# The last 64 tokens of two batches as one chunk of a gating product, with loads and splits in other places

## The chip, the cores and the metric

The kernel runs on one core of a Trainium2 chip. The metric is the device time of one execution in microseconds, as the median over several runs. Before the change it is 576.93 us (three runs, 575.62 to 577.12).

## What is computed

An attention (4 batches, 8 heads, 576 tokens, 64 dimensions, rotary embedding), then two feed-forward layers over the concatenated heads, in float32:

```python
attn = softmax(rot(q) @ rot(k).T / sqrt(64)); x = attn @ v        # (4, 576, 512)
h = gelu_tanh(x @ w_in)                                           # w_in (512, 1024)
u, v = h[..., :512], h[..., 512:]
v_n = (v - mean) / sqrt(var + 1e-6) * g_ln                        # per token
v_s = einsum('ts,bsd->btd', w_sg, v_n) + b_sg[None, :, None]      # mixes the 576 tokens
x2 = x + (u * v_s) @ w_out
gate = sigmoid(causal_conv5(x2) * conv_w)
out = (gate * (x2 @ w_val)) @ w_out2
```

The weights of both layers come as 64-bit floats, which the kernel narrows itself.

## The kernel before, in words

**Precision.** A product in float32 is made of three products of a faster type: each operand is split into a high part (a cast on ScalarE, ACT) and a low part (source minus high part, on GpSimd, POOL, or the Vector engine, DVE), and high x high, high x low and low x high are summed in PSUM. `split` (line 255) records such a pair, `tt` (line 246) one subtraction or product on DVE ("D") or POOL ("P"), `acopy` one cast.

**Order.** Nothing is emitted at once. `Plan.add` collects tasks with an engine, an estimated cost and the keys they read and write; `Plan.order` then runs a list scheduler over them, by due time, and emits the instructions in the order that it finds. Each engine takes its own instructions in that order, one after the other. TensorE's order is fixed by the order of recording. `after=` adds a dependence: `sp[i]` is the first TensorE task of pair i's phase, `mq[i]` the DMA that stores the row maxima of pair i. Loads and stores go through one queue, SP's.

**Attention** works on 16 pairs of heads, four per batch. `phase(i)` interleaves nine score units of pair i (exponentials on ACT, lines 495 to 508) with the nine score units for the maxima of pair i+1 (line 445, reduced by DVE on line 447 into `mx`, and on line 461 into `mn`). Behind it come the product with v (lines 526 and 536, read out as `xu`) and the sums of exponentials (line 562, read out by ACT as `ss`). `prep_high(i+2)` makes the rotary products on DVE (`raw`) and casts `qp`, `qh`, `kh` on ACT; `prep_low` makes `ql` and `kl` on POOL. The unnormalised result goes to `xu_d[i]` and the reciprocal sums to `r_d[i]` in DRAM.

Beside the pairs 4 to 14 lies what the next stage needs: `weights_a` loads eight pieces of w_in, narrows each with one ACT and four DVE operations (lines 295 to 302) and splits it, and splits five pieces of w_sg (`s_h`, `s_l`) that go through the buffers `xs`. `x_prep(0)`, from pair 13 on, loads four row blocks of x of batch 0 into `xs`, multiplies with the reciprocal sums (`rb`) on POOL, stores them as `x_d` and splits them into `XH`, `XL`. Two `xs` buffers serve in turn.

**Gating** (`part_a`, once per batch): v units, u units, g units.
- Three v units multiply chunks of 128 tokens of x with the right half of w_in (line 686): chunks 0 and 1, chunks 2 and 3, and one last chunk. 576 is 4 x 128 + 64, so the last chunk takes the last 128 tokens, of which the first 64 were done already. Each chunk costs 12 matmuls of 512 columns. Then gelu, the statistics (DVE, with one power on POOL), normalisation and the split into `vn`; of the last chunk only its upper 64 rows, as high and low part in the two halves of one tile `t4`.
- Four u units (line 725) do the left half, by blocks of 128 channels.
- Four g units (lines 739 and 742) do the mixing over tokens. DVE adds the bias (`vs`), POOL multiplies with u, and the result goes to `g_d`.

`x_prep(b + 1)` is recorded between the u and g units: `XH` and `XL` exist once, so the next batch's can only be written when the u units have read them.

**Second layer.** `x2_part` (line 804) makes x2 in tiles `xs` and `rb`, splits it (`xh2`, `xl2`) and runs the convolution (four DVE operations on line 822 per block). `val_part` (line 837) and `out_part` (line 866) follow, batch by batch.

Of the kernel before, what the change touches and what calls it, by code (L numbers as in the profile page):

```python
# [10 lines left out]
F32 = mybir.dt.float32  # L11
# [155 lines left out]
def mixer_kernel(ctx: ExitStack, tc: tile.TileContext, qk, v, vrem, cs, w_in, g_ln, w_sgT, b_sg,  # L167
# [42 lines left out]
    s_l = pA.tile([128, 5, S], F32R, name="s_l")  # L210
    WR = tiles(pA, "wr", 1, [128, 512, 2], I32)
# [107 lines left out]
    def weights_a():  # L319
        for hf in (1, 0):  # L320
            for k in range(4):
                cc = slice(512 * hf, 512 * hf + 512)
                weight64(f"win{k}_{hf}", lambda k=k, cc=cc: w_h[:, k, cc], lambda k=k, cc=cc: w_l[:, k, cc],
                         w_in[128 * k:128 * k + 128, 1024 * hf:1024 * hf + 1024], [mq[4 + nw[0]]])
# [6 lines left out]
        for k in range(5):  # L331
            xs = XS[k % 2][:, 4:]

            def ld(q, k=k, xs=xs):
                if k < 4:
                    q.dma_start(out=xs, in_=w_sgT[128 * k:128 * k + 128, :])
                else:
                    q.dma_start(out=xs[0:64], in_=w_sgT[512:576, :])
                    q.dma_start(out=xs[64:128], in_=w_sgT[512:576, :])
            dma(288, ld, w=[("xs", k % 2)], n=1 + (k == 4), after=[mq[5 + 2 * k]])  # L340
            split(lambda k=k: s_h[:, k], lambda k=k: s_l[:, k], lambda xs=xs: xs, S, [("xs", k % 2)],
                  ("sg", k, "h"), ("sg", k, "l"), after=[sp[5 + 2 * k]])
# [232 lines left out]
    sp = []  # L575
# [7 lines left out]
    def attention():  # L583
# [42 lines left out]
        for i in range(NPAIR):  # L626
# [26 lines left out]
    def x_prep(b):  # L653
        for hp in range(4):
# [4 lines left out]
            op = [mq[13 + hp // 2]]  # L659
# [9 lines left out]
            tt("P", xs, xs, lambda rb=rb: rb, ALU.mult, S, [("rb", hp % 2)], [kx], [sp[14]] if not b else ())  # L669
            dma(290, lambda q, xs=xs, i=i: q.dma_start(out=x_d[i], in_=xs()), [kx], [("x_d", i)])  # L670
            split(lambda hp=hp: XH[:, hp], lambda hp=hp: XL[:, hp], xs, S, [kx], ("X", hp, "h"), ("X", hp, "l"), "D")

    def part_a(b):
# [4 lines left out]
        for c0 in (0, 2, 4):  # L678
            cs_ = (c0, c0 + 1) if c0 < 4 else (4,)

            def mm(ps, cs_=cs_):
                for y, c in enumerate(cs_):
                    o = 128 * c if c < 4 else S - 128
                    for k in range(4):
                        for z, (p, q) in enumerate(three(3)):
                            nc.tensor.matmul(ps[:, y], X[p][:, k, o:o + 128], Wm[q][:, k, 512:1024], start=k == z == 0,  # L686
                                             stop=k == 3 and z == 2)
            ps, kp = unit(12 * 0.233 * len(cs_), mm, [*xk, *[(f"win{k}_1", m) for k in range(4) for m in hl]])
# [5 lines left out]
            for y, c in enumerate(cs_):  # L694
# [315 lines left out]
```

## Time and profile before

| | |
|---|---|
| median of three runs | 576.93 us |
| time of the profiled execution | 575.71 us |
| its span, first to last instruction | 573.8 us |
| TensorE (PE) busy | 560.6 us, 98% |
| DVE busy | 396.2 us, 69% |
| ACT busy | 277.0 us, 48% |
| POOL busy | 254.1 us, 44% |
| share of the chain that ended last: PE, DVE, DMA | 90%, 5%, 2% |
| stages: attention, gating, second layer | to 252, to 418, to the end |

Busy time says how long an engine had an instruction in work. Whether a saving on it is a saving of time is read from the chain: the work that ended last, followed back from the end, at each step to what released it. Idle time of an engine ahead of an instruction stands in brackets with its releaser.

### The profile page before, as it was taken

The page shows a single profiled execution, that of the slowest core. Times are in us where ns is not written, and L with a number is a line of the kernel's source. Part 1 is how long each engine was busy: PE and PEld are TensorE (multiplying, and loading weights), DVE is VectorE, ACT ScalarE, POOL GpSimd, SP SyncE. Part 2 cuts the span into 40 slices and gives each one's busy share as a digit, 9 for nine tenths or more (in the row PEclk, how much of TensorE's full clock was granted, in tenths as well). Part 3 has the DMA queues.
Part 4 walks back from the last instruction along what each step waited for, and adds up shares of the span by engine and source line. Part 5 has one row for each costly group of instructions (what it writes and reads, how often), then busy time and mean ns, then how long its engine had stood idle before and what let it go on. Part 6 is the DMA issues. An engine that isn't in the chain of part 4 may idle for free.

```text
span 573.8 us, 11977 instructions
## 1 busy us (share of the span) xinstructions
PE 560.6 (98%) x4682; PEld 470.4 (82%) x4682; DVE 396.2 (69%) x584; ACT 277.0 (48%) x448; POOL 254.1 (44%) x211
## 2 busy tenths in 40 slices
PE   7899999999999999999999999999999999999996
PEld 4677777677776676768989989989999989899985
DVE  5677777888889889726457665656568998837720
ACT  2565666666666666634425325325335453433321
POOL 5633333445545445564577477547453222220200
PEclk9899999999999999999999999999999999999999
DMA  5735556655656555553383472451513341220102
GB/s 210 205 95 133 149 140 194 190 127 170 183 158 182 156 149 153 179 152 115 100 283 106 153 245 79 155 166 39 178 62 125 104 138 39 81 94 1 38 37 93
DMA packets 53832, 76.79 MB, mean 134 GB/s; under 512 B 25104, under 2 KB 29712, under 8 KB 53776
## 3 DMA queue, kind: packets, MB, share of 16 engines
q1 hardware_dynamic: 53632, 76.03, 43.7%
q8 instruction: 37, 0.61, 0.4%
q14 instruction: 19, 0.16, 0.1%
q10 hardware_dynamic: 144, 0.00, 0.0%
HBM read 55.33 MB, written 18.95 MB: 129 GB/s over the span
## 4 chain that ended last, share of the span: by engine, by line
PE 90%; DVE 5%; DMA 2%; issue 1%; ACT 1%; POOL 0%; SPq 0%; DVEq 0%; ACTq 0%
PE ps L495 11%; PE ps L526 10%; PE ps L686 10%; PE ps L837 9%; PE ps L725 9%; PE ps L804 9%; PE ps L739 9%; PE ps L866 9%; PE ps L562 5%; PE ps L445 4%; PE ps L503 3%; DVE raw L249 2%; DVE mx L447 2%; PE ps L742 1%; PE ps L536 1%
## 5 line engine op out<-in xcount | busy, mean ns | idle before, releaser
L447 DVE TENSOR_REDUCE mx<-ps 128x2 f32<-128x576 f32 x128 | 91.1, 754 | 39.3 <-PE ps L445 21.7
L508 ACT ACTIVATE e<-ps 128x576 f32<-128x576 f32 x144 | 86.2, 651 | 25.8 <-PE ps L503 16.3
L250 POOL TENSOR_TENSOR ql<-raw,qh 128x576 fp32r<-128x576 f32 x15 | 21.7, 1445 | 101.3 <-ACT qh L253 68.2
L526 PE MATMUL ps<-e,vm 128*64 128x288 f32 x512 | 65.6, 409 | 0.0
L739 PE MATMUL ps<-s_h,vn 128*128 128x288 f32 x256 | 56.0, 294 | 0.0
L526 PEld LDWEIGHTS ps<-e,vm 128*64 128x64 f32 x512 | 35.4, 137 | 24.7 <-issue 2.5
L250 POOL TENSOR_TENSOR ac<-e,e 128x576 f32<-128x576 f32 x32 | 45.0, 1428 | 15.1 <-ACT e L508 15.1
L249 DVE TENSOR_TENSOR raw<-raw,cst 128x1152 f32<-128x1152 f32 (+2 forms) x35 | 43.2, 1243 | 6.5 <-DMA cst<-cs 6.5
L445 PE MATMUL ps<-kh,qp 64*128 64x288 f32 x256 | 39.2, 340 | 4.5 <-ACT qp L253 2.7
L739 PEld LDWEIGHTS ps<-s_h,vn 128*128 128x128 f32 x256 | 42.8, 188 | 0.0
L495 PE MATMUL ps<-qh,kh 64*128 64x288 f32 x256 | 39.2, 301 | 1.2 <-DVE mx L447 1.2
L250 POOL TENSOR_TENSOR vs<-vs,u 128x576 f32<-128x576 f32 x16 | 27.1, 1691 | 28.3 <-DVE vs L746 24.4
L495 PE MATMUL ps<-qh,kl 64*128 64x288 f32 x256 | 38.4, 295 | 0.0
L495 PE MATMUL ps<-ql,kh 64*128 64x288 f32 x256 | 38.4, 295 | 0.0
L495 PE MATMUL ps<-mr,one_r 64*128 64x288 f32 x256 | 38.3, 293 | 0.0
L445 PEld LDWEIGHTS ps<-kh,qp 64*128 64x128 f32 x256 | 22.9, 186 | 18.6 <-ACT qh L253 5.6
L725 PE MATMUL ps<-XH,w_l 128*128 128x288 f32 x128 | 37.8, 295 | 0.0
L837 PE MATMUL ps<-xh,wh_v 128*128 128x288 f32 x128 | 37.8, 295 | 0.0
L837 PE MATMUL ps<-xh,wl_v 128*128 128x288 f32 x128 | 37.8, 295 | 0.0
L739 PE MATMUL ps<-s_l,vn 128*128 128x288 f32 x128 | 37.7, 295 | 0.0
L725 PE MATMUL ps<-XL,w_h 128*128 128x288 f32 x128 | 37.7, 295 | 0.0
L837 PE MATMUL ps<-xl,wh_v 128*128 128x288 f32 x128 | 37.7, 295 | 0.0
(155 smaller groups left out, 1599.2 us busy)
## 6 DMA issues: line engine op xcount, KB each, us to landing
raw<-qk SPq DMA_DIRECT2D x31, 576.0 KB
xu_d<-xu SPq DMA_DIRECT2D x32, 144.0 KB
rb<-r_d SPq DMA_DIRECT2D x32, 144.0 KB
xs<-xu_d SPq DMA_DIRECT2D x16, 288.0 KB
x_d<-xs SPq DMA_DIRECT2D x16, 288.0 KB
g_d<-vs SPq DMA_DIRECT2D x16, 288.0 KB
vm<-v SPq DMA_DIRECT2D x16, 256.0 KB
wr<-w_in SPq DMA_DIRECT2D x8, 512.0 KB
```

The lines of the kernel that those rows point to most:

```text
L249: return add("DVE", dve(n), lambda: nc.vector.tensor_tensor(out_(), a(), b(), op), r, w, after, lock=True)
L250: return add("Pool", pool(n), lambda: nc.gpsimd.tensor_tensor(out_(), a(), b(), op), r, w, after, lock=True)
L445: nc.tensor.matmul(ps[:, h, 0:HALF], QP[j2][rows, c], kh[rows, cols], start=True, stop=True)
L447: add("DVE", 0.76, lambda: nc.vector.tensor_reduce(out=MX[j2][:, hk, :, c], in_=ps[:, :, 0:HALF], axis=AX.X, op=ALU.max), [kps], [("mx", j ...
L495: nc.tensor.matmul(ps[:, h, 0:HALF], x[rows, keys] if o < 3 else x[rows], y[rows, cols], start=o == 0, stop=o == 3)
L508: add("Act", 0.62, lambda: nc.scalar.activation(E[n], ps[:, :, 0:HALF], AF.Exp), [kps], [("e", n)])
L526: nc.tensor.matmul(pv[64 * hf:64 * hf + 64, h, 0:HALF], VM[j2][:, j, h], E[EU[i, us[hf]]][:, h], start=j == 0, stop=False, skip_group_chec ...
L686: nc.tensor.matmul(ps[:, y], X[p][:, k, o:o + 128], Wm[q][:, k, 512:1024], start=k == z == 0, stop=k == 3 and z == 2)
L725: nc.tensor.matmul(ps[:, hf, 0:HALF], Wm[p][:, k, dc], X[q][:, k, cols], start=k == z == 0, stop=k == 3 and z == 2)
L739: nc.tensor.matmul(ps[:, hf, 0:HALF], VN()[p][:, k, dc], SG[q][:, k, cols], start=k == z == 0, stop=False)
L804: nc.tensor.matmul(ps[:, hf, 0:HALF], w2("o", p)[:, k, dc], (T["gh"], T["gl_"])[q][j][:, k, cols], start=k == z == 0, stop=k == 3 and z == 2)
L837: nc.tensor.matmul(ps[:, hf, 0:HALF], w2("v", p)[:, k, dc], (T["xh2"], T["xl2"])[q][j][:, k, cols], start=k == z == 0, stop=k == 3 and z == 2)
```

## The change

- Batches 0 and 1 share one last v chunk of 128 tokens, the last 64 of each, and so do batches 2 and 3. It is multiplied in the even batch; the odd batch has two v units. Its operands are new tiles `XR` (high and low), made by `xr_prep`: eight loads of 128x64 from `xu_d`, sixteen of 64x64 of `r_d`, a product and a subtraction on POOL and a cast on ACT. `xr_prep(0)` runs beside the attention, `xr_prep(2)` within batch 0.
- `t4` becomes two tiles, one for each batch of the couple: four casts and two POOL subtractions in an even batch instead of two and one in each.
- The pieces of w_in are loaded from pairs 2, 3, 5, 6, 8, 9, 11, 12 instead of 4 to 11, those of w_sg from 4, 6, 7, 9, 10 instead of 5, 7, 9, 11, 13.
- `x_prep(0)` starts its row blocks from pairs 11, 12, 13 and 14 instead of 13, 13, 14 and 14.
- The low part of x2 is made by DVE in batches 0 and 1, and by POOL, as before, in batches 2 and 3.

```diff
+    XR = [pA.tile([128, 4, 128], F32R, name=f"xr_{nm}") for nm in "hl"]
+    RR = pA.tile([128, 4, 128], F32, name="rr")
...
-                         w_in[128 * k:128 * k + 128, 1024 * hf:1024 * hf + 1024], [mq[4 + nw[0]]])
+                         w_in[128 * k:128 * k + 128, 1024 * hf:1024 * hf + 1024], [mq[(2, 3, 5, 6, 8, 9, 11, 12)[nw[0]]]])
...
-            dma(288, ld, w=[("xs", k % 2)], n=1 + (k == 4), after=[mq[5 + 2 * k]])
+            dma(288, ld, w=[("xs", k % 2)], n=1 + (k == 4), after=[mq[(4, 6, 7, 9, 10)[k]]])
...
             phase(i)
+            ep.append(P.last_pe)
...
-            op = [mq[13 + hp // 2]]
+            op = [mq[11 + hp]]
...
-            split(lambda hp=hp: XH[:, hp], lambda hp=hp: XL[:, hp], xs, S, [kx], ("X", hp, "h"), ("X", hp, "l"), "D")
+            split(lambda hp=hp: XH[:, hp], lambda hp=hp: XL[:, hp], xs, S, [kx], ("X", hp, "h"), ("X", hp, "l"), "D", [ep[11 + hp]] if not b else ())
+
+    def xr_prep(b):
+
+        def f():
+            return XR[1].bitcast(F32)
+        for m in range(2):
+            for hp in range(4):
+                i, cc = 4 * (b + m) + hp, slice(64 * m, 64 * m + 64)
+                op = [] if b else [mq[9 + hp]]
+                dma(32, lambda q, i=i, hp=hp, cc=cc: q.dma_start(out=f()[:, hp, cc], in_=xu_d[i][:, 512:576]), [("xu_d", i)],
+                    [("xr", m, hp)], [*op, *P.readers.get(("XR", "l"), ())])
+
+                def ld(q, i=i, hp=hp, cc=cc):
+                    for h in range(2):
+                        q.dma_start(out=RR[64 * h:64 * h + 64, hp, cc],
+                                    in_=r_d[i][S * h + 512:S * h + S].partition_broadcast(64))
+                dma(32, ld, [("r_d", i)], [("rr", m, hp)], op, n=2)
+        parts = [(m, hp) for m in range(2) for hp in range(4)]
+        tt("P", lambda: RR, f, lambda: RR, ALU.mult, 512, [("xr", *x) for x in parts], [("rr", *x) for x in parts], [] if b else [sp[12]])
+        keys = [("rr", *x) for x in parts]
+        acopy(lambda: XR[0], lambda: RR, 512, keys, [("XR", "h")])
+        tt("P", lambda: XR[1], lambda: RR, lambda: XR[0].bitcast(F32), ALU.subtract, 512, [("XR", "h"), *keys],
+           [("XR", "l"), *[("xr", *x) for x in parts]], [] if b else [sp[13]])
...
-        for c0 in (0, 2, 4):
+        for c0 in (0, 2, 4)[:3 - b % 2]:
...
-                    o = 128 * c if c < 4 else S - 128
...
-                            nc.tensor.matmul(ps[:, y], X[p][:, k, o:o + 128], Wm[q][:, k, 512:1024], start=k == z == 0,
+                            nc.tensor.matmul(ps[:, y], X[p][:, k, 128 * c:128 * c + 128] if c < 4 else XR[p][:, k], Wm[q][:, k, 512:1024], start=k == z == 0,
...
+                    for m in range(2):
+                        own, other = slice(64 * m, 64 * m + 64), slice(64 - 64 * m, 128 - 64 * m)
+                        for rows in (own, other):
+                            acopy(lambda m=m, rows=rows: T4()[m][rows], lambda gi=gi, own=own: GL()[gi][own, 0], 512, [("gl", gi, y), kg],
+                                  [("vn", 4 + m, "h" if rows is other else "l")])
+                        tt("P", lambda m=m, own=own: T4()[m][own], lambda gi=gi, own=own: GL()[gi][own, 0],
+                           lambda m=m, own=own: T4()[m][own].bitcast(F32), ALU.subtract, 512, [("gl", gi, y), kg], [("vn", 4 + m, "l")])
...
+        if b == 0:
+            xr_prep(2)
...
-                  ("X2", j, dd, "h"), ("X2", j, dd, "l"))
+                  ("X2", j, dd, "h"), ("X2", j, dd, "l"), "D" if b < 2 else "P")
```

The scheduler makes a new order of all this. At three places it reads as follows.

ScalarE at the end of pair 13's phase, two before the last, before the change: the casts of the last pair (`qp`, `qh`, `kh`) with the readout `xu`, and `ss`, the readout of the sums.

```order
L253 CAST w_h<-wf_142 128x512
L508 ACTIVATE e_188<-ps_121 128x576
L253 CAST qp_160<-raw_146 128x512
L253 COPY xu_192<-ps_124 128x576
L253 CAST qh_147<-raw_146 128x576
L253 CAST kh_153<-raw_146 128x576
L566 ACTIVATE ss_193<-ps_123 128x288
L295 ACTIVATE wt_143<-wr_141 128x512
```

And the same place of the changed kernel:

```order
L297 ACTIVATE wt_201<-wr_199 128x512
L510 ACTIVATE e_191<-ps_121 128x576
L255 CAST qp_163<-raw_149 128x512
L255 COPY xu_195<-ps_124 128x576
L255 CAST qh_150<-raw_149 128x576
L255 CAST XH<-xs_133 128x576
L568 ACTIVATE ss_196<-ps_123 128x288
L255 CAST kh_156<-raw_149 128x576
L510 ACTIVATE e_183<-ps_124 128x576
```

A cast of x stands ahead of `ss`, and `kh` behind it.

DVE in the last phase with score units for a next pair (stretch 14 in the prediction), before: from the reduction on line 461 to the first reductions of the last pair.

```order
L461 TENSOR_REDUCE mn_174<-mx_172 128x8
L455 TENSOR_REDUCE mn_174<-ps_122 128x1
L249 TENSOR_TENSOR raw_146<-raw_146,cst 128x1152
L249 TENSOR_TENSOR raw_146<-raw_146 128x576
L249 TENSOR_TENSOR raw_146<-raw_146,cst 128x1152
L249 TENSOR_TENSOR raw_146<-raw_146 128x576
L300 SCALAR_TENSOR_TENSOR wt_198<-wr_196,wt_198 128x512
L302 SCALAR_TENSOR_TENSOR wf_197<-wr_196,wt_198 128x512
L447 TENSOR_REDUCE mx_173<-ps_121 128x2
```

The same place of the changed kernel:

```order
L463 TENSOR_REDUCE mn_177<-mx_175 128x8
L251 TENSOR_TENSOR raw_149<-raw_149,cst 128x1152
L457 TENSOR_REDUCE mn_177<-ps_122 128x1
L251 TENSOR_TENSOR raw_149<-raw_149 128x576
L251 TENSOR_TENSOR raw_149<-raw_149,cst 128x1152
L573 RECIPROCAL rc_197<-rc_197 128x9
L251 TENSOR_TENSOR raw_149<-raw_149 128x576
L251 TENSOR_TENSOR XL<-xs_134,XH 128x576
L251 TENSOR_TENSOR XL<-xs_133,XH 128x576
L449 TENSOR_REDUCE mx_176<-ps_121 128x2
```

Two subtractions of x take the place of the two weight operations, and a reciprocal has come between.

POOL in batch 0 of the gating, before: the last `vn` subtraction, t (the last 64 tokens' low part) and the first g product `vs`.

```order
L702 TENSOR_TENSOR st_3293<-st_3293,mhalf 128x1
L250 TENSOR_TENSOR vn_3285<-gl_3289,vn_3284 128x512
L250 TENSOR_TENSOR t_3286<-gl_3288,t_3286 64x512
L250 TENSOR_TENSOR wl_o<-wf_142,wh_o 128x512
L250 TENSOR_TENSOR vs_3290<-vs_3290,u 128x576
```

The same place of the changed kernel:

```order
L727 TENSOR_TENSOR st_3342<-st_3342,mhalf 128x1
L252 TENSOR_TENSOR vn_3333<-gl_3338,vn_3332 128x512
L252 TENSOR_TENSOR rr<-xr_l,rr 128x512
L252 TENSOR_TENSOR t_0_3334<-gl_3337,t_0_3334 64x512
L252 TENSOR_TENSOR t_1_3335<-gl_3337,t_1_3335 64x512
L252 TENSOR_TENSOR wl_o<-wf_145,wh_o 128x512
L252 TENSOR_TENSOR xr_l<-rr,xr_h 128x512
L252 TENSOR_TENSOR vs_3339<-vs_3339,u 128x576
```

The product and the subtraction for the chunk of batches 2 and 3 have come in, ahead of t and ahead of `vs`.

## Rows read from the trace of the kernel before

**Rows 1.** Busy time by stretch, the gating (columns as headed).

```profile
core 0: us, PE busy (x) PEld busy (x) DVE busy (x) ACT busy (x) POOL busy (x), PEclk, DMA share, GB/s
...
252.00:418.00 166.00, 166.00 (x1075) 155.46 (x1073) 97.78 (x160) 62.36 (x97) 98.37 (x78) 1.00 0.46 148
```

**Rows 2.** Chain that ended last, by time (start us, us, what): gating, second layer.

```profile
252.01 14.14 PE ps L686 x60
...
278.88 1.60 PE ps L739 x12
...
293.72 13.94 PE ps L686 x60
...
320.38 1.60 PE ps L739 x12
...
437.27 12.97 PE ps L837 x96
```

**Rows 3.** Timeline of DVE, line 461 (start us, us, engine, operation): cuts between stretches.

```profile
101.87 0.17 DVE L461 TENSOR_REDUCE mn<-mx 128x8 fp32r<-128x16 f32 x1
...
116.52 0.17 DVE L461 TENSOR_REDUCE mn<-mx 128x8 fp32r<-128x16 f32 x1
...
130.74 0.17 DVE L461 TENSOR_REDUCE mn<-mx 128x8 fp32r<-128x16 f32 x1
...
145.50 0.17 DVE L461 TENSOR_REDUCE mn<-mx 128x8 fp32r<-128x16 f32 x1
...
173.96 0.17 DVE L461 TENSOR_REDUCE mn<-mx 128x8 fp32r<-128x16 f32 x1
...
189.04 0.17 DVE L461 TENSOR_REDUCE mn<-mx 128x8 fp32r<-128x16 f32 x1
...
203.46 0.17 DVE L461 TENSOR_REDUCE mn<-mx 128x8 fp32r<-128x16 f32 x1
...
217.68 0.17 DVE L461 TENSOR_REDUCE mn<-mx 128x8 fp32r<-128x16 f32 x1
...
232.75 0.17 DVE L461 TENSOR_REDUCE mn<-mx 128x8 fp32r<-128x16 f32 x1
```

**Rows 4.** Timeline of DVE, stretches 13 and 14.

```profile
210.62 1.43 DVE L447 TENSOR_REDUCE mx<-ps 128x2 f32<-128x576 f32 x2 [1.05 <-PE ps L445]
...
218.43 2.08 DVE L249 TENSOR_TENSOR raw<-raw,cst 128x1152 f32<-128x1152 f32 x1
...
224.00 1.80 DVE L302 SCALAR_TENSOR_TENSOR wf<-wr,wt 128x512 int32<-128x512 int32 x1
```

**Rows 5.** Timeline of POOL, stretch 14 and gating.

```profile
223.69 1.56 POOL L250 TENSOR_TENSOR ql<-raw,qh 128x576 fp32r<-128x576 f32 x1 [4.39 <-ACT qh L253]
...
255.76 1.43 POOL L250 TENSOR_TENSOR xs<-xs,rb 128x576 f32<-128x576 f32 x1 [4.48 <-DMA xs<-xu_d]
...
273.17 1.50 POOL L250 TENSOR_TENSOR vn<-gl,vn 128x512 fp32r<-128x512 f32 x1
...
275.81 1.29 POOL L250 TENSOR_TENSOR t<-gl,t 64x512 fp32r<-64x512 f32 x1 [1.13 <-ACT t L711]
...
311.42 2.73 POOL L250 TENSOR_TENSOR vn<-gl,vn 128x512 fp32r<-128x512 f32 x2
```

**Rows 6.** Timeline of ScalarE, stretches 6 and 14.

```profile
109.02 0.67 ACT L253 CAST s_h<-xs 128x576 fp32r<-128x576 f32 x1
109.58 0.67 ACT L295 ACTIVATE wt<-wr 128x512 f32<-128x512 f32 x1
...
224.52 0.41 ACT L566 ACTIVATE ss<-ps 128x288 f32<-128x288 f32 x1 [0.33 <-ACT kh L253]
```

**Rows 7.** Tile vr: issues on SP (ns), then its landing on the chain.

```profile
L431 SPq DMA_DIRECT2D vr<-vrem x16: 328/334/1260, 14.3 to 222.4; - x16
...
49.57 1.68 DMA vr<-vrem
```

**Rows 8.** Timeline of DVE, second layer: gate products with and without POOL beside them.

```profile
431.62 4.68 DVE L822 SCALAR_TENSOR_TENSOR gt<-xs,cw,gt 128x576 f32<-128x576 f32 x4
...
466.62 3.72 DVE L822 SCALAR_TENSOR_TENSOR gt<-rb,cw,gt 128x576 f32<-128x576 f32 x5
```

More of the change, by code (lines that the diff above doesn't have):

```diff
@@ L668, in x_prep @@
             dma(290, ld, [("r_d", i)], [("rb", hp % 2)], n=2)
[L669 removed]
+            tt("P", xs, xs, lambda rb=rb: rb, ALU.mult, S, [("rb", hp % 2)], [kx], [sp[11 + hp]] if not b else ())
             dma(290, lambda q, xs=xs, i=i: q.dma_start(out=x_d[i], in_=xs()), [kx], [("x_d", i)])
[L671 removed]
+            split(lambda hp=hp: XH[:, hp], lambda hp=hp: XL[:, hp], xs, S, [kx], ("X", hp, "h"), ("X", hp, "l"), "D", [ep[11 + hp]] if not b else ())
[19 more added lines that the diff above has]
+           [("XR", "l"), *[("xr", *x) for x in parts]], [] if b else [sp[13]])
     def part_a(b):
@@ L682, in mm @@
                 for y, c in enumerate(cs_):
-                    o = 128 * c if c < 4 else S - 128
                     for k in range(4):
                         for z, (p, q) in enumerate(three(3)):
-                            nc.tensor.matmul(ps[:, y], X[p][:, k, o:o + 128], Wm[q][:, k, 512:1024], start=k == z == 0,
+                            nc.tensor.matmul(ps[:, y], X[p][:, k, 128 * c:128 * c + 128] if c < 4 else XR[p][:, k], Wm[q][:, k, 512:1024], start=k == z == 0,
                                              stop=k == 3 and z == 2)
-            ps, kp = unit(12 * 0.233 * len(cs_), mm, [*xk, *[(f"win{k}_1", m) for k in range(4) for m in hl]])
+            ps, kp = unit(12 * 0.233 * len(cs_), mm, [*(xk if c0 < 4 else [("XR", m) for m in hl]), *[(f"win{k}_1", m) for k in range(4) for m in hl]])
             gi = c0 // 2 % 2
@@ L741, in mm @@
                     for z in range(2):
-                        nc.tensor.matmul(ps[:, hf, 0:HALF], T4()[0][:, dc], SG[z][:, 4, cols], start=False, stop=z == 1)
-            ps, kp = unit(28 * PASS, mm, [("vn", c, m) for c in range(5) for m in hl] + [("sg", c, m) for c in range(5) for m in hl])
+                        nc.tensor.matmul(ps[:, hf, 0:HALF], T4()[b % 2][:, dc], SG[z][:, 4, cols], start=False, stop=z == 1)
+            ps, kp = unit(28 * PASS, mm, [("vn", c, m) for c in (0, 1, 2, 3, 4 + b % 2) for m in hl] + [("sg", c, m) for c in range(5) for m in hl])
             y = dd % 2
@@ L896, in close_att @@
         T["vn"] = [pa2.tile([128, 4, DM], F32R, name=f"vn{j}") for j in range(2)]
-        T["t4"] = [pa2.tile([128, DM], F32R, name="t4")]
+        T["t4"] = [pa2.tile([128, DM], F32R, name=f"t4_{m}") for m in range(2)]
         T["u"] = [pa2.tile([128, 4, S], F32, name="u")]
@@ L904, in mixer_kernel @@
     weights_a()
+    xr_prep(0)
     x_prep(0)
@@ L908, in mixer_kernel @@
         [("gl", x) for x in range(2)] + [("gl", x, y) for x in range(2) for y in range(2)] + [("vs", x) for x in range(2)]
-        + [("st", x) for x in range(3)] + [("u", x) for x in range(4)] + [("vn", x, m) for x in range(5) for m in "hl"])})
+        + [("st", x) for x in range(3)] + [("u", x) for x in range(4)] + [("vn", x, m) for x in range(6) for m in "hl"])})
     n0 = len(P.tasks)
```

9 lines of the change are left out of this document (2 added, 7 removed).

## The prediction, on record before the result

> **What bounds the kernel now.** I read the profile from the outside in. First the busy time by stretch: from 252 to 418 us, the gating stage that the change cuts, TensorE is busy for all of its 166.00 us, at a granted clock of 1.00, the upper of its two levels (2.4 GHz) [rows 1]. Nothing else is: the Vector engine (DVE) has 97.78 us of work there and GpSimd (POOL) 98.37. So in this stage an instruction taken off TensorE is time taken off the kernel, as long as no other engine becomes the later one.
>
> Then the chain that ended last. It runs through TensorE nearly everywhere, and a batch of the gating reads off as pieces [rows 2]: the 60 matmuls of the first product of batch 1 last 13.94 us, the u units follow until 320.38, and the four g units end where batch 2 begins. Between the pieces there is no gap.
>
> The attention ahead of it is bound by TensorE too, but not without loss. I cut it at the reduction on line 461, which stands once in each pair's stretch [rows 3]; stretch i is that of `phase(i)`. An undisturbed stretch lasts 14.22 us (116.52 to 130.74). Stretch 6 lasts 14.65, 8 lasts 14.76, 11 lasts 15.08, 12 lasts 14.42 and 14 lasts 15.07. These five lose 0.43 + 0.54 + 0.86 + 0.20 + 0.85 = **2.88 us** against 14.22. The change moves exactly the work that stands in them, so each loss needs its cause.
>
> Stretches 11 and 14: the eight score reductions on line 447 free the PSUM tiles for TensorE, and in a good stretch the first of them starts 210.62 - 203.46 = 7.16 us after the cut, having waited 1.05 us for TensorE [rows 3, 4]. In stretch 14 DVE has rotary work and the last two weight operations to do before it. The rotary product took 2.08 us and the weight operation on line 302 took 1.80, ending 225.80 - 217.68 = 8.1 us after the cut: about 0.9 too late [rows 3, 4]. During the second of them POOL was in a subtraction of its own, from 223.69 on [rows 5]; what that does to DVE is seen again where x's low part comes up, below. Stretches 6 and 8: ScalarE has two casts ahead of the exponentials (109.02 and 109.58 in stretch 6) [rows 6], which makes the first exponential, and so a PSUM tile, late.
>
> **The change part by part.**
>
> *The shared chunk.* Batches 1 and 3 lose their third unit of 12 matmuls; batches 0 and 2 keep theirs, on other operands. A matmul of this shape costs 13.94 / 60 = 0.2323 us on the chain [rows 2], so 24 of them are **-5.58 us**. The cover of what hangs on them: in batch 1 the last vn was ready at 314.15 and the g units began at 320.38 [rows 2, 5]. The u units now start right behind the second unit, whose end lies 2.79 us (12 matmuls) before the third's; vn depends on that second unit alone, so 6.23 - 2.79 = 3.4 us of cover are left. The shared chunk's normalisation drops out there too. I cost this at nothing.
>
> *The chunk's operands, batches 2 and 3.* `xr_prep(2)` is issued in batch 0: SP issues eight 128x64 loads once the first chunk has been multiplied (252.01 + 14.14 = 266.15) [rows 2]; POOL's product `rr` waits for them and now stands ahead of both t subtractions. The nearest rows are the loads of `vr`, of the same size: 0.334 us to issue and 1.68 from issue to landing, as the chain has it [rows 7]. Eight issues and one landing end at 266.15 + 2.7 + 1.7 = 270.5. POOL is busy with vn until 274.67 and did t at 275.81 to 277.10 [rows 5]. With `rr` between (1.50 us, as the vn subtraction of that size) t_0 ends at 274.67 + 1.50 + 1.29 = 277.5, and g begins at 278.88 [rows 2, 5]. So it is hidden, with 1.4 us left. From below it can give nothing, since TensorE does not wait there now; from above, see the second rival. The other `rr`, its cast and its subtraction lie in attention and delay nobody: they wait behind the additions of the exponentials.
>
> *Weights and w_sg earlier, x from pair 11 on.* No weight operation is added or removed; they get other neighbours. Read from the new order: no stretch has two casts ahead of the exponentials any more, which gives back 0.43 + 0.54. The pattern of stretches 11 and 14 (two casts before the last exponential, POOL's two subtractions behind them, then two-input weight operations ahead of the first reduction) now stands in stretches 6 and 9. I price it as before, 2 x 0.86 and once 0.20 for the stretch after it: 1.92, for 1.91 removed. New are stretches 13 and 14. In 13 one x subtraction stands in the middle of the eight reductions. It costs nothing if it fits into their idle time, 0.74 at DVE's free pace for this size [rows 8], and 1.8 if it meets POOL as line 302 did [rows 4]; I take **0.7**, nearest to the middle one. In 14, kh of the last pair is cast behind `ss`, which reads the sums that TensorE finishes right before that pair's scores. `ss` started at 224.52, 0.33 us after the end of the kh cast, and took 0.41; a cast of 0.67 behind it ends at 225.6 instead of 224.2, and TensorE was ready at 224.5 [rows 6]. The scores of the last pair wait for it: **1.1** (0.9 to 1.6; the two x subtractions on DVE fall into the same wait). Attention then loses 1.92 + 0.7 + 1.1 = 3.72 instead of 2.88, **+0.84**.
>
> *x's low part on DVE for batches 0 and 1.* Eight subtractions leave POOL for a DVE that is nearly full there. Rows: four gate products took 4.68 us (1.17 each) while POOL ran its subtractions, five took 3.72 (0.74 each) with POOL idle [rows 8]. At DVE's free pace four subtractions cost 4 x 0.74 = 3.0 and give back up to 4 x 0.43 = 1.7. In the new order one gate product and three subtractions stand between the last sum of batch 0 (431.62) and the end of its x: 434.6 at 0.74 each, 436.3 at 1.17; the value product began at 437.27 [rows 2, 8]. I take 0, between -0.2 and +0.8. The Trainium skill, "SBUF — State Buffer", Who interferes with whom, says that a DVE instruction with two SBUF inputs and a GpSimd one that reads SBUF exclude each other for a whole instruction. The trace agrees (1.17 against 0.74). By it the lower end, 434.6, holds and the move is free; if 1.17 were DVE's own pace, the upper end would hold and leave 1.0 us.
>
> **The sum**, against the profiled execution (span 573.8, its time 575.71): 575.71 - 5.58 + 0.84 = 571.0. That execution lies near the lowest of the three runs shown, 1.2 below their median of 576.93, so I add a third of that: **571.4 us**.
>
> **The rivals.**
>
> 1. *The new waits in attention don't come.* The motif did not strike in every stretch that has it, and weights now have free stretches between them. Then the 2.88 go as well: 575.71 - 5.58 - 2.88 + 0.4 = 567.7. Against it: the cast of kh behind `ss` stands in the order. Chance 0.13 for anything under 569.5.
> 2. *The small loads are late and hold POOL in batch 0.* `rr` heads POOL's queue, t_0, t_1, a weight and the g products stand behind it. The loads may be 4.2 (274.7 - 270.5) + 1.4 = 5.6 us late; each us beyond is one at TensorE, and the gain of 5 is gone at 10 us, about 576. For it: POOL and SP take their work in order, and eight loads must all have landed. Against it: 1.68 us for one [rows 7]. The Trainium skill, "DMA: Bandwidth & Descriptors", Specifications, holds that transfers under 512 B lose line rate, and these rows have 256 B; `vr` has the same rows and shows no such loss. Chance 0.08 for a result within 0.3%, this and the next together.
> 3. *x's part on DVE makes DVE the bound of the second stage, or the x chain costs more in stretches 12 to 15.* 1 to 3 us more: 572.5 to 575. Chance 0.13 for 573.5 to 575.2.
> 4. *Slower: the x chain holds ScalarE.* XH of x's third and fourth row block now stands in ScalarE's queue ahead of `ss` and kh of stretch 14, and ahead of the eviction `xu`. Each waits on a load, a POOL product, and an x buffer that DVE frees late: the load can go out when DVE has done three reductions and a subtraction, some 10 us into stretch 13; with the 4.48 us that POOL once waited for such a load, its product of 1.43 [rows 5] and a cast of 0.67 it ends at 16.6, and `ss` is due 14.22 + 6.84 = 21.1 after the same cut. So it decides from 4.5 us of lateness on: two such chains 8 us late would cost 2 x 3.5 = 7.0 and give 578.4. No row shows a load that late. Chance 0.04.
>
> **How the numbers follow.** A measurement of this kernel can tell about 0.3% (1.7 us) from no change. The forecast (569.5 to 573.5) has 0.62; rivals 1 and 3 add 0.13 each, all of them faster by more than 0.3% (below 575.2): 0.88. Same 0.08, slower 0.04. The range takes in the bounds above (stalls from 0.97 less to about 2 more, the second stage up to 0.8) and most of rivals 1 and 3: 568.4 to 574.2, leaving out about 2 in 10.
>
> **What would show it.** Right: 216 matmuls of the first product instead of 240, 24 of them on `xr`; batches 1 and 3 starting u after some 11.15 us, g units without a gap, stretches 6 and 9 near 15.1, stretch 14 about 1 us too long with ScalarE's kh as what TensorE waits for. Wrong: a gap ahead of a g unit with POOL's t as the releaser, DVE ahead of TensorE on line 837's operands, or attention that is shorter than now.

## The result and the profile after

The changed kernel takes **582.0 us** (median of eight runs, 578.08 to 583.38) against 576.66 for the kernel before: a ratio of **1.008, 95% interval 1.0051 to 1.011**. 571.4 was forecast; it is slower.

The profiled execution has a span of 581.6 us, 7.8 more than before; it is the slowest of the eight, and by the medians the loss is 5.3. The busy time by stretch shows where the loss is not; first the gating, then the second layer (stretch, sum, then each engine, granted clock, DMA share, GB/s):

```profile
265.76:426.18 160.42, 160.42 (x1050) 151.07 (x1051) 97.02 (x152) 61.42 (x95) 96.05 (x76) 1.00 0.45 143
426.18:581.60 155.42, 150.82 (x984) 141.95 (x983) 105.13 (x149) 59.98 (x101) 16.33 (x11) 0.99 0.23 75
```

The gating lasts 160.42 us instead of the 166.17 between the starts of its first product (252.01) and of the second layer (418.18): 5.75 less, with TensorE busy for all of it. The second layer lasts 155.42 instead of 573.8 - 418.18 = 155.62. So all of the loss is in the attention, which ends at 265.76 instead of 252.01.

2.46 us of these 13.75 lie ahead of the second cut (32.88 instead of 30.42) and are not the change's. TensorE's granted clock fell to its lower level, 1.2 GHz, earlier in the start of this execution; in the kernels below the second cut comes between 30.1 and 32.8 us, whatever the edit. Busy time of 2 us, after, then before:

```profile
16.00:18.00 2.00, 2.00 (x6) 0.86 (x4) 1.30 (x2) 0.00 (x0) 1.92 (x2) 0.50 0.50 85
```

```profile
16.00:18.00 2.00, 2.00 (x10) 1.44 (x11) 2.00 (x4) 0.00 (x0) 1.92 (x2) 1.00 0.51 86
```

11.3 us are left, and the cuts tell where. Timeline of DVE after, the reduction that is line 461 of before, stretches 11 to 14 [rows 3]:

```profile
177.69 0.17 DVE L463 TENSOR_REDUCE mn<-mx 128x8 fp32r<-128x16 f32 x1
193.98 0.17 DVE L463 TENSOR_REDUCE mn<-mx 128x8 fp32r<-128x16 f32 x1
209.78 0.17 DVE L463 TENSOR_REDUCE mn<-mx 128x8 fp32r<-128x16 f32 x1
225.75 0.17 DVE L463 TENSOR_REDUCE mn<-mx 128x8 fp32r<-128x16 f32 x1
246.51 0.17 DVE L463 TENSOR_REDUCE mn<-mx 128x8 fp32r<-128x16 f32 x1
```

| stretch | 3 | 6 | 8 | 9 | 11 | 12 | 13 | 14 |
|---|---|---|---|---|---|---|---|---|
| before | 14.23 | 14.65 | 14.76 | 14.22 | 15.08 | 14.42 | 14.22 | 15.07 |
| forecast | 14.22 | 15.08 | 14.22 | 15.08 | 14.22 | 14.22 | 14.92 | 15.32 |
| after | 14.71 | 15.07 | 14.21 | 15.07 | 16.29 | 15.80 | 15.97 | 20.76 |

Stretches 6, 8 and 9 came out to 0.01 us. Stretches 11 to 14 are 10 us longer than before. What TensorE waits for in the attention has names that it did not have before (engine, line, tile; us in total, times, longest):

```profile
PE ps L447 <- ACT kh L255: 4.0, 1, 4.0
PE ps L447 <- DVE mx L449: 1.6, 1, 1.6
PE ps L497 <- DMA mr<-mn: 1.6, 2, 1.2
```

`mr` are the row maxima, which three small transfers carry from DVE's result to where TensorE multiplies with them. The chain that ended last goes through them, and then through x (start us, us, what):

```profile
208.59 5.36 DMA raw<-qk
...
214.01 4.47 DMA mr<-mn
...
218.53 1.66 PE ps L497 x16
...
224.53 8.87 issue
...
233.43 1.41 POOL xs L252
...
234.86 0.04 ACT XH L255
...
235.44 0.40 ACT ss L568
235.84 0.57 ACT kh L255
```

Why `mr` and x are late is seen in SP's timeline of stretches 13 and 14. The maxima are ready at 209.78 + 0.17, but the queue stands at stores, a load of x, a weight and two of the new small loads (`rr`), and issues `mr` at 214.01, 4.2 us after the cut. In the last 0.6 us of these SP issued nothing: by the chain above it stood for the landing of the `raw` load of 208.59, which it had issued eight issues earlier:

```profile
210.50 0.62 SPq L666 DMA_DIRECT2D xs<-xu_d  x1
211.22 0.44 SPq L574 DMA_DIRECT2D r_d<-rc  x1
211.70 0.50 SPq L315 DMA_DIRECT2D wr<-w_in  x1
212.24 1.14 SPq L689 DMA_DIRECT2D rr<-r_d  x2
214.01 1.16 SPq L471 DMA_DIRECT2D mr<-mn  x2
...
218.38 1.23 SPq L689 DMA_DIRECT2D rr<-r_d  x2
...
227.82 1.12 SPq L670 DMA_DIRECT2D rb<-r_d  x2
229.03 0.54 SPq L666 DMA_DIRECT2D xs<-xu_d  x1
229.62 1.38 SPq L684 DMA_DIRECT2D xr_l<-xu_d  x3
```

Before, after the cut at 203.46, SP issued them 0.2 us later and had idle time ahead of it:

```profile
202.69 0.56 SPq L572 DMA_DIRECT2D r_d<-rc  x1
203.66 1.17 SPq L469 DMA_DIRECT2D mr<-mn  x2
205.59 0.59 SPq L472 DMA_DIRECT2D mr<-mn  x1
```

The durations of all SP rows sum to 15.2, 14.7, 14.4 and 18.7 us in stretches 11 to 14, against 12.6, 9.8, 10.4 and 10.0 before (a row of several issues includes the time between them).

The row maxima are not the only small result in this queue. The sums of exponentials go through it to DVE as `rc`, and DVE takes their reciprocal ahead of score reductions. In stretch 11 it stood 2.44 us for them, with the last four reductions behind, and TensorE then 1.6 us for `mx`. Before, it did not wait. Timeline of DVE, stretch 11, after, then before:

```profile
191.12 0.22 DVE L573 RECIPROCAL rc<-rc 128x9 f32<-128x9 f32 x1 [2.44 <-DMA rc<-ss]
191.25 2.70 DVE L449 TENSOR_REDUCE mx<-ps 128x2 f32<-128x576 f32 x4
```

```profile
184.51 0.20 DVE L571 RECIPROCAL rc<-rc 128x9 f32<-128x9 f32 x1
```

And the wait of 4.0 us in stretch 14 cost more than itself: behind it TensorE's granted clock was at its lower level until 242 us. Busy time of 236 to 242 us and of the whole stretch 14 after, then of stretch 14 before:

```profile
236.00:242.00 6.00, 5.55 (x46) 5.55 (x48) 3.10 (x5) 2.88 (x5) 2.71 (x3) 0.50 0.50 118
225.75:246.51 20.76, 16.78 (x164) 12.68 (x166) 12.55 (x18) 9.65 (x16) 9.78 (x7) 0.84 0.58 140
```

```profile
217.68:232.75 15.07, 14.45 (x164) 10.18 (x166) 13.75 (x18) 10.39 (x18) 9.58 (x8) 1.00 0.54 140
```

The same 164 matmuls kept TensorE busy for 16.78 instead of 14.45 us: 2.3 of the 5.7 us that stretch 14 lost are the clock's.

### The profile page after: what moved, and what is told of

Read it like the earlier page. It is cut to its first block, busy times and chain, and to the rows that moved or that the text cites. A ratio compares the mean times of both kernels' runs of the same rounds, so it can differ in the third digit from the quotient of the medians.

```text
span 581.6 us, 11978 instructions
## 1 busy us (share of the span) xinstructions
PE 561.9 (97%) x4658; PEld 470.4 (81%) x4658; DVE 396.8 (68%) x584; ACT 277.3 (48%) x448; POOL 242.3 (42%) x205
## 4 chain that ended last, share of the span: by engine, by line
PE 82%; DMA 7%; DVE 5%; issue 4%; ACT 1%; POOL 1%; SPq 0%; DVEq 0%; ACTq 0%; POOLq 0%
PE ps L497 10%; PE ps L752 9%; PE ps L833 9%; PE ps L866 9%; PE ps L766 9%; PE ps L711 9%; PE ps L895 8%; PE ps L528 7%; PE ps L447 4%; PE ps L564 3%; DMA mr<-mn 2%; DVE raw L251 2%; PE ps L505 2%; DVE mx L449 2%; DMA raw<-qk 2%
## 5 line engine op out<-in xcount | busy, mean ns | idle before, releaser
L252 POOL TENSOR_TENSOR ac<-e,e 128x576 f32<-128x576 f32 x32 | 46.5, 1474 | 14.6 <-ACT e L510 14.6
L447 PE MATMUL ps<-kh,qp 64*128 64x288 f32 x256 | 41.0, 351 | 9.4 <-ACT kh L255 5.5
L497 PE MATMUL ps<-mr,one_r 64*128 64x288 f32 x256 | 40.7, 301 | 1.6 <-DMA mr<-mn 1.6
L497 PE MATMUL ps<-qh,kh 64*128 64x288 f32 x256 | 40.9, 308 | 1.2 <-DVE mx L449 1.2
L497 PE MATMUL ps<-qh,kl 64*128 64x288 f32 x256 | 39.8, 301 | 0.0
L497 PE MATMUL ps<-ql,kh 64*128 64x288 f32 x256 | 39.8, 300 | 0.0
L752 PE MATMUL ps<-XH,w_h 128*128 128x288 f32 x128 | 37.7, 294 | 0.0
```

What stands on the lines that cost most here:

```text
L252: return add("Pool", pool(n), lambda: nc.gpsimd.tensor_tensor(out_(), a(), b(), op), r, w, after, lock=True)
L447: nc.tensor.matmul(ps[:, h, 0:HALF], QP[j2][rows, c], kh[rows, cols], start=True, stop=True)
L497: nc.tensor.matmul(ps[:, h, 0:HALF], x[rows, keys] if o < 3 else x[rows], y[rows, cols], start=o == 0, stop=o == 3)
L752: nc.tensor.matmul(ps[:, hf, 0:HALF], Wm[p][:, k, dc], X[q][:, k, cols], start=k == z == 0, stop=k == 3 and z == 2)
```

## The experiments

Three theories stood at the start. **Queue:** the 24 small loads of the chunk for batches 0 and 1 fill SP's queue. **Chain:** x from pair 11 on puts its casts ahead of `ss` and `kh` on ScalarE. **Neighbours:** weights and x subtractions on DVE delay the score reductions. "Attention" in the table is the time from the second cut to the first u matmul of batch 0, in the profiled execution, less the 235.57 us of before; it leaves the start out. The medians of before beside these runs were 576.3 to 577.0. One execution need not be like the median: the profiled one was the lowest of its run in runs 4, 7, 10, 13 and 14, and the slowest in run 11.

| run | us | ratio, 95% interval | attention |
|---|---|---|---|
| the change | 582.0 | 1.008 [1.0051, 1.011] | +11.2 |
| without the chunk | 579.27 | 1.004 [1.0019, 1.0061] | +3.4 |
| chunk alone | 578.38 | 1.0018 [0.9995, 1.004] | +7.2 |
| small loads from pair 3 on | 578.91 | 1.0037 [1.0008, 1.0066] | +7.2 |
| small loads merged | 576.23 | 1.0003 [0.9976, 1.0029] | +4.2 |
| 24 loads alone | 579.93 | 1.0052 [1.0027, 1.0077] | +3.9 |
| 24 loads, few rows | 578.04 | 1.0018 [0.9999, 1.0038] | +2.3 |
| chunk alone, merged and late | **569.83** | **0.9873 [0.9846, 0.9901]** | -0.1 |
| the change, merged and late | 574.57 | 0.9955 [0.9928, 0.9982] | +3.1 |
| the change, x as before | 577.57 | 1.0006 [0.9981, 1.003] | +5.9 |
| the change, kh ahead of x | 578.63 | 1.0033 [1.0016, 1.0051] | +6.1 |
| chunk alone, loads behind the maxima | 578.88 | 1.0036 [1.001, 1.0061] | +8.5 |
| new weights alone | 577.28 | 1.0011 [0.9993, 1.0029] | +0.8 |
| 24 loads alone, on GpSimd | 578.15 | 1.0022 [1.0002, 1.0043] | +0.7 |
| chunk alone, loads on GpSimd | 574.82 | 0.9968 [0.995, 0.9986] | +2.1 |
| merged, late, low part on DVE | 570.82 | 0.9891 [0.9859, 0.9924] | -0.3 |
| chunk's three operations alone | 576.51 | 0.9998 [0.9976, 1.002] | +0.5 |

**1. Without the chunk.** The change with three v units in each batch, no `xr_prep`, and the old last chunk.

```diff
-        for c0 in (0, 2, 4)[:3 - b % 2]:
+        for c0 in (0, 2, 4):
...
-    xr_prep(0)
```

> The change without the shared chunk and its 24 small loads; weights, x from pair 11 on and the low part on DVE stay as changed. Queue theory (the small loads fill SP's queue, which issues 14.4 to 18.7 us of loads in stretches 11 to 14, and everything behind them is late): those stretches fall back to at most 15.3 us each, batch 0 of the gating starts within 4 us of the 252.0 of before, and the time is 576.7 to 580. Chain theory (the casts of x in ScalarE's queue ahead of ss and kh do it, since x starts at pair 11): stretch 14 stays above 18 us, and the time is 583 to 588, the 5.6 us of the chunk on top of the changed kernel. Neighbour theory (weights and x subtractions on DVE beside the reductions): stretches 11 to 13 stay near 16, time 582 to 585.

579.27, stretch 14 at 15.55. The chain theory falls as the main cause. But 3.0 us of loss are there without any small load: the neighbours are a second cost, larger than forecast (0.84).

**2. The chunk alone.** All five other edits of the change undone.

> The kernel before with the shared chunk alone: weights, pieces of w_sg, x and the low part of x2 at their old places. Queue theory: the 24 small loads cost wherever SP's queue is near its limit; with 12.56, 9.82, 10.43 and 9.98 us of issues in stretches 11 to 14 before and some 3 us more in each, stretch 11 goes above 15.6 us and the others stay under 15; time 572 to 576. Chain theory: no cast of x stands early, so the whole gain comes: 571 to 571.6. Neighbour theory: the same, 571 to 571.6.

578.38, stretch 11 at 18.59. Slower than the queue theory gave, and far from the 571 of the other two: the chunk costs more in the attention than it gives in the gating. From the first u matmul to the end it takes 1.6 us more than run 7; there the value product of batch 0 waited 1.3 us for DVE, which had gate products to do first. The change itself, with the low part on DVE, has no such wait, but neither has run 7, with the low part on POOL: it goes with the order of instructions that runs 2, 11 and 14 got.

**3. The small loads earlier.**

```diff
-                op = [] if b else [mq[9 + hp]]
+                op = [] if b else [mq[max(i + 2, 3)]]
```

> The changed kernel with the small loads of each pair issued two pairs after it (pairs 3 to 9) instead of pairs 9 to 12. Queue theory: stretches 3 to 9 have 2 to 4 us of SP's time free each and 24 issues are 12.7 us over seven of them, so little is late there, and stretches 11 to 14 fall to 15 us or less: 571.5 to 575. Chain theory: stretch 14 stays above 18 us and the time at 579 or above. Neighbour theory: stretches 11 to 13 near 16, 578 to 581.

578.91: a miss. The mean free time of a stretch is no measure. In stretch 4 (16.66 us) the loads stand between the cut and `mr` again, which is issued 4 us after the cut. In stretch 13 (18.06) TensorE waited 2.3 us for `kh` and was then at the lower clock (0.50 from 219 to 222 us); why `kh` was late I have not isolated.

**4. The small loads merged**: `xu_d` and `r_d` as one tensor per batch, so that one load serves four pairs.

```diff
+            dma(128, lambda q, m=m, cc=cc: q.dma_start(out=f()[:, :, cc], in_=xu_b[b + m][:, :, 512:576].rearrange("a p c -> p a c")),
...
+                    q.dma_start(out=RR[64 * h:64 * h + 64, :, cc],
+                                in_=r_b[b + m][:, S * h + 512:S * h + S].partition_broadcast(64))
```

> The changed kernel with the small loads of four pairs as one: 6 issues for each chunk instead of 24, with the same bytes in the same rows of 256 B. Queue theory, if it is the time that SP takes to issue: 18 x 0.55 = 9.9 us of the queue come back, stretches 11 to 14 fall to 15.3 us or less, time 571 to 574.5. If it is the number of small rows that the transfers move and not the issues, stretches 11 to 13 stay near 16 and the time above 578. Chain theory: stretch 14 stays above 18 us, 579 or above.

576.23, 5.8 less than the change with the same rows of 256 B. That it is above the range fits the 3 us of the neighbours, which I had not counted. A load of four pairs took SP 0.62 us (median), one of a single pair 0.59.

**5. The 24 loads alone**, added to the kernel before with nothing that uses them but the due time of the third v unit of batch 0.

> The kernel before, with the shared chunk's 24 small loads of the attention added at the places that they have with the chunk alone, and nothing else: no product, no cast, no subtraction, three v units in every batch. The chunk alone came out at 578.4, which is 7.7 us above 576.3 - 5.58. Queue theory: the loads alone cost all of that, 576.3 + 7.7 = 584 (582 to 586), with stretch 11 above 17 us. If the product on POOL, the cast or the subtraction were what costs, the loads alone leave the time at 576 to 578.

579.93: the loads alone cost 3.2 us, less than half of what I expected, 3.9 in the attention. Stretches 11 to 13 are 16.48, 15.43 and 16.30.

**6. The same loads with few rows.**

```diff
-                    q.dma_start(out=RR[64 * h:64 * h + 64, hp, cc],
-                                in_=r_d[i][S * h + 512:S * h + S].partition_broadcast(64))
+                    q.dma_start(out=RR[64 * h:64 * h + 4, hp, cc],
+                                in_=r_d[i][S * h + 512:S * h + S].partition_broadcast(4))
```

> As the run with the 24 loads alone, but each load moves 8 rows of 256 B, or 4, instead of 128 or 64: the same number of issues in the same places with a sixteenth of the rows. If the places in SP's queue are what costs (0.35 to 0.6 us of each issue, ahead of the row maxima that TensorE waits for), and an issue does not get shorter with fewer rows, the time is as in that run, 582 to 586. If it is the rows in the transfer queues, it is 576 to 579. If the issues get shorter with the rows, it lies between, by their measured length.

The issues of `rr` on SP (ns minimum, median, maximum), with 64 rows, then with 4:

```profile
L688 SPq DMA_DIRECT2D rr<-r_d x16: 485/595/717, 160.6 to 213.4; - x16
```

```profile
L688 SPq DMA_DIRECT2D rr<-r_d x16: 246/292/488, 162.4 to 213.5; - x16
```

Half the issue time (7.0 instead of 13.1 us for all 24, with `xr_l` at 0.293 instead of 0.445), and 2.3 instead of 3.9 us of attention: the cost goes with the issue time and not with the rows, which went to a sixteenth. But both moved, so run 13 was needed.

**7. The chunk alone, merged and late**: run 2 with the loads of run 4, allowed from the last pair on.

```diff
-            op = [] if b else [mq[9 + m]]
+            op = [] if b else [mq[15]]
```

> The shared chunk alone, weights, w_sg, x and x2's low part as before, with its loads merged to 6 issues and allowed only from the last pair on, where no row maxima follow behind them. Queue theory: stretches 1 to 14 lose the 2.9 us of before and no more, and the whole gain comes: 576.3 - 5.6 = 570.7 (570 to 572). Should the loads hold up the loads of x for batch 0 in the last stretch instead, batch 0 starts up to 3 us later there: 573.7. Chain theory or neighbour theory alone: 571 as well, as nothing of x or the weights has moved.

**569.83**, 1.3% faster than before, and faster than both kernels. Its chain has the gating where before had it (252.01), and the short odd batch:

```profile
251.91 14.06 PE ps L712 x60
...
293.52 11.14 PE ps L712 x48
```

**8. The change, merged and late.**

> The changed kernel with the same merged and late loads: all its other parts (weights, w_sg, x from pair 11 on, low part on DVE) stay. The change without the chunk took 3.0 us more than the kernel before. Queue theory with the other parts as a second, separate cost: 576.3 - 5.6 + 3.0 = 573.7 (572.7 to 574.7). If the chain theory holds by itself, stretch 14 stays above 18 us and the time above 578; if all of the loss was the loads, 570.7 to 571.5.

574.57, as forecast for two separate costs, queue and neighbours: this is the change without the first.

**9. The change with x at its old places.**

```diff
-            op = [mq[11 + hp]]
+            op = [mq[13 + hp // 2]]
```

> The changed kernel with x at its old places (pairs 13 and 14, products from pair 14 on, no wait on the end of a phase); the 24 small loads and the new weights stay. If the 9 us that stretches 11 to 14 lose are the loads and the chain of x together (x's third row block is loaded late through the full queue, its cast stands ahead of ss and kh, and TensorE waits 4 us in stretch 14), then stretch 14 falls from 20.8 to 15 to 16 us and the time to 582.0 - 5 = 577 (575.5 to 578.5). If the queue alone makes stretch 14 long, it stays above 18 us and the time above 580.

577.57; stretch 14 falls from 20.76 to 14.23. Stretch 13 went to 17.69, though, and its chain shows the queue theory in one piece: behind DVE's maxima four issues of SP, and then the transfer (start us, us, what):

```profile
208.99 0.47 SPq L574
...
209.51 0.49 SPq L315
...
210.05 0.51 SPq L689
...
210.60 0.59 SPq L689
...
211.29 5.90 DMA mr<-mn
```

Line 689 is the small load, 315 a weight, 574 a store. TensorE waited 1.5 us for `mr` there, and its clock was at 0.50 from 218 to 221 us.

**10. The change with kh of the last pair ahead of x's later casts** on ScalarE (their casts recorded as following it).

> The changed kernel, loads and x where they are, but x's second, third and fourth cast may stand on ScalarE only behind the cast of kh of the last pair. If the cast of x ahead of ss and kh is what holds TensorE in stretch 14 (chain theory, for this stretch), stretch 14 falls to 16 us or less and the time to 577 to 578.5. If kh or ss are late for another reason (their loads or the queue), stretch 14 stays above 18 us and the time within 1.5 of 582.

578.63, 3.4 less; stretch 14 at 17.08, between the two expectations. The cast of x ahead of `kh` is a real cause, but a follow-up: without a full queue (run 8) the same order costs 1.34 us there (15.56).

**11. The chunk alone, its 24 loads behind the maxima**, three in each of stretches 3 to 10, forced ahead of the next load of v.

> The shared chunk alone with all 24 small loads, unmerged, three for each of the stretches 3 to 10, placed so that they are issued behind a stretch's row maxima (and ahead of the next load of v) and none stands ahead of the next row maxima. If the harm is only in standing ahead of the row maxima, stretches 3 to 10 stay as before and the time is 570.7 to 572. If 24 issues and their rows cost wherever they stand, since the rotary loads and kr stand behind them now, some stretches go above 15 us and the time is 573 to 578.

578.88: standing behind the maxima doesn't help. In stretch 6 (17.79), rotary loads, a load of v and stores stand between the cut at 105.39 and `mr`, which is issued 2.4 us after it; its first issue then took 3.2 us where 0.5 is usual, for which the trace shows no cause. The chain:

```profile
107.79 6.52 DMA mr<-mn
114.31 0.04 issue
114.36 1.63 PE ps L508 x18
```

**12. The new weights alone.**

> The kernel before with the weights and w_sg at their new places alone. The change without the chunk lost 0.69, 0.55, 0.85 and 0.85 us in stretches 3, 4, 6 and 9 and 0.84, 1.23 and 1.33 in 12 to 14. If the first four are the weights' and the last three x's, then stretches 3, 4, 6 and 9 are as there, 8, 11 and 12 are at 14.2, and the time is 575.5 to 577, within 1 us of before. If the weights made the last three too, it is 578 to 580.

577.28. Stretches 3, 4, 6 and 9 take 14.65, 15.01, 15.07 and 15.06, stretch 12 15.05, stretches 8, 11, 13 and 14 14.23 at most. So stretch 12 was the weights' too; without the chunk, 13 and 14 (15.45, 15.55) were x's.

**13 and 14. The loads from GpSimd's queue**, alone and with the chunk.

```diff
+    def dma_p(kb, fn, r=(), w=(), after=(), n=1):
+        return add("Pool", 0.3 * n, lambda: fn(nc.gpsimd), r, w, after, lat=1.8 + kb / 200.0, kb=kb)
```

> The kernel before with the 24 small loads alone, as in the run on the loads alone (579.9 against 576.8), but issued by GpSimd's queue instead of SP's, at the same pairs. The bytes, rows and destinations are the same; only SP's places are free. If SP's time is what they cost, stretches 8 to 14 are as before and the time is 576.5 to 577.5. If the rows in the transfer engines cost, it is 579 to 581. If issuing takes POOL's time from ql, kl and the additions, some other stretch goes above 15.5 us with POOL as what is waited for.

The same 24 transfers now cost 0.7 us of attention instead of 3.9 in the profiled executions, and 1.1 us instead of 3.2 by the medians, whose intervals overlap. Issues on GpSimd (ns), and their landing:

```profile
L691 POOL DMA_DIRECT2D rr<-r_d x16: 516/526/704, 145.3 to 205.1; - x16
...
DMA to landing us min/median/max: 4.1/4.8/5.3
```

So most of what they cost is SP's time, and little their rows. The Trainium skill, "DMA: Bandwidth & Descriptors", Issuing engines are not separate DMA queues, says that starting DMAs on several engines saves only the sequencer's time for initiating them, usually little beside the DMA. For one transfer the trace agrees (0.53 us to issue, 4.1 to 5.3 to landing). But 24 issues ahead of small results that TensorE needs were not little: 3.2 of 3.9 us of attention went with SP's part.

> The shared chunk alone, weights, x and low part as before, its small loads issued by GpSimd's queue (those of batch 0 for batches 2 and 3 too). If SP's time is all that the loads cost, 576.8 - 5.6 = 571.2 (570.5 to 572), against 578.4 with the loads on SP. If the rows cost, 574 to 576.

574.82, 3.6 less than run 2 with the loads on SP, but not the 571.2 expected if SP's time were all; it lies in the range named for the rows. The trace has other causes for most of the gap: the wait of 1.3 us in the second layer of run 2, and in stretch 13 (15.76) one that is new. POOL's product `rr` waits for the last small load, and the cast of the chunk stands ahead of `kh` on ScalarE, for which TensorE waits 1.5 us:

```profile
209.46 1.58 POOL L255 TENSOR_TENSOR rr<-xr_l,rr 128x512 f32<-128x512 f32 x1 [2.56 <-DMA xr_l<-xu_d]
...
211.07 0.62 ACT L258 CAST xr_h<-rr 128x512 fp32r<-128x512 f32 x1 [1.02 <-POOL rr L255]
211.60 0.67 ACT L258 CAST kh<-raw 128x576 fp32r<-128x576 f32 x1
```

**15. Run 7 with the low part of x2 on DVE.**

```diff
-                  ("X2", j, dd, "h"), ("X2", j, dd, "l"))
+                  ("X2", j, dd, "h"), ("X2", j, dd, "l"), "D" if b < 2 else "P")
```

> The version with merged late loads and everything else at its old place (569.8) with the low part of x2 on DVE for batches 0 and 1 added: what this part of the change does by itself. Forecast: nothing, 569.6 to 570.6 (-0.2 to +0.8). If DVE were the bound of the second layer: 571 or more.

570.82, against 569.83; the intervals overlap. From the first u matmul to the end it takes 301.85 us, run 7 301.99: no effect, as forecast.

**16. The chunk's product, cast and subtraction alone**, on zeros, in the kernel before.

> The kernel before with the shared chunk's product, cast and subtraction in the attention, but without its loads: two memsets on GpSimd, in pairs 7 and 8, give them zeros to work on, and the third v unit is made of x as before. With the loads on SP the chunk alone lengthened the attention by 7.2 us, the loads alone by 3.9. If the three operations cost the difference by themselves, the time is 578 to 580 and stretches 12 to 14 are longer; if they are covered, as forecast, it is 576.5 to 577.5 and the difference lies in the two together.

576.51 beside 576.43: on operands that lie ready they are covered. The loads alone and the operations alone add 3.9 and 0.5 us to the attention, the chunk alone 7.2 in its profiled execution. Of the other 2.8 us, 2.1 lie in stretch 11 (18.59 against 16.48), before any operation of the chunk has run. DVE stood longer for `rc` there, in the chunk alone, then in the loads alone, and in the chunk alone TensorE's clock fell behind it:

```profile
189.03 0.22 DVE L573 RECIPROCAL rc<-rc 128x9 f32<-128x9 f32 x1 [3.66 <-DMA rc<-ss]
```

```profile
186.92 0.21 DVE L573 RECIPROCAL rc<-rc 128x9 f32<-128x9 f32 x1 [1.77 <-DMA rc<-ss]
```

```profile
192.00:195.00 3.00, 3.00 (x15) 2.23 (x15) 2.96 (x5) 0.65 (x1) 1.26 (x1) 0.50 0.96 230
```

Why `rc` was later with the same loads stays open; it may be the spread of one execution (the chunk alone ran from 575.95 to 580.21).

## Why the prediction was wrong

- **The shared chunk, -5.58: right.** The gating is 5.75 us shorter; batch 1's first product took 11.14 us for 48 matmuls.
- **The operands for batches 2 and 3, hidden: right.** `rr` ran from 287.42, both t were done at 288.86 + 3.10 = 291.96, and the g units began at 292.54 without a wait. Rival 2 did not come, though the eight `xr_l` loads took 4.27 us on SP where 2.7 were reckoned; waits for TensorE's last unit lie in between.
- **"The other `rr`, its cast and its subtraction lie in attention and delay nobody": this step failed.** The three operations delayed nobody in this kernel, where the cast came at 247.42, behind the last maxima, nor in run 16; with late loads they can (run 14). But the step priced only operations of POOL and ScalarE, and the loads in front of them not at all: 16 x 0.595 + 8 x 0.445 = 13.1 us of SP's queue (run 5's medians), in stretches that had 2 to 5 us free. In its place the runs showed small results, `mr` and `rc`, late behind these loads, at 3.9 us of attention by themselves (run 5) and 0.7 when GpSimd issues them (run 13). The row for an issue was at hand [rows 7] and was used for batch 0 alone, where it did not matter.
- **Rival 4 had the mechanism of the largest single wait, and the wrong size.** It let x's third load go out some 10 us into stretch 13; it went out at 229.03, 19.3 us into it, behind the full queue. The product followed at 233.43, the casts XH, `ss` and `kh` behind that, and TensorE stood for 4.0 us; the lower clock behind it, 2.3 us more, was in no term. Runs 9 and 10 take 4.4 and 3.4 us of the time away from two sides. 0.04 was too little: the lateness was asked of rows that had no full queue.
- **Weights, 1.92 for the 2.88 of before, so -0.96: too low.** Stretches 6 and 9 came to 15.07 as priced and stretch 8 fell to 14.21, but stretches 3, 4 and 12 pay as well, which the prediction put at nothing: +0.8 instead of -0.96 (run 12).
- **x in stretches 13 and 14, +1.8: somewhat low without the queue** (15.45 and 15.55 in run 1, so 1.23 + 1.33 = 2.6). The wait for `kh` that it priced at 1.1 is there in run 1, with 1.1 us.
- **x2's low part on DVE, 0: right** (run 15; the second layer is 0.2 us shorter). The last subtraction of batch 0's x ended at 441.01 + 1.42 = 442.4, 2.8 us ahead of the value product at 445.26.

The sum against the trace: -5.75 - 0.20, +2.46 of the start, +11.3 of attention make 7.8; of the 11.3, 0.84 were forecast. Run 8 puts 3.1 of them on weights and x; the rest comes with the small loads, by themselves (3.9) and through the x chain that they make late (runs 9 and 10), with the 2.3 us of the clock behind it. That gating and second layer came out as forecast was no luck, each being a term of the sum.

## What to carry to other kernels

Count every transfer that a step issues as work of the engine that issues it, and add it up per stage as for a compute engine: here SP had 2 to 5 us free in 14. Then ask what is queued behind it: small results that other engines wait for (the row maxima, the sums) go through the same queue. Merge small loads, and put them where nothing urgent follows: the same chunk, alone, gives 7.0 us (run 7, 569.83 against 576.78) instead of taking 2.1 (run 2, not clear of noise).

## What the runs showed of the hardware that was not expected

- An issue cost SP about the same whether it moved 64 rows of 256 B (0.59 us, run 5) or four times as many (0.62, run 4); with 4 rows it was 0.29 (run 6). One issue for four pairs is three issues saved.
- The 2 KB of `mr` took 4.47 to 6.52 us from issue to landing on the chains above. That is no effect of the new loads: by the times at which their semaphores rose in the trace of the kernel before, its `mr` transfers took 1.9 to 5.8 us. What changed is when they were issued: in stretch 13 the first one landed 8.7 us after the cut instead of 3.7.
- A wait of TensorE can cost more than its length. Its granted clock was at the lower level behind a wait of 4.0 us in the changed kernel, 3.0 in run 2, 2.3 in run 3 and 1.5 in run 9. Behind one of 1.7 us in run 4 and of 1.5 in run 14 it stayed at 1.00; what decides that, no run here shows.
- The Trainium skill, "DMA: Bandwidth & Descriptors", Specifications, names 512 B as the least transfer for line rate. Rows below that are not what cost most here: the same rows of 256 B cost 0.7 us of attention when GpSimd issued them and 3.9 when SP did.
